# Attention and channel mix in one kernel: the token mixtures as a four-chunk difference, scalings by mu spread over three engines, and a four-chunk addition

## The chip, the core and the metric

The kernel runs on one core of a Trainium2 chip. Its engines are TensorE (PE, with its weight loads shown as PEld), VectorE (DVE), ScalarE (ACT), GpSimd (POOL) and SyncE (SP), which here only issues DMAs. The metric is the device time of one execution in microseconds (us), as the median of several runs. One further execution was recorded by the profiler; every row of a profile below is from such an execution, and its times count from the first instruction.

## What is computed

First a windowed attention over 4 batches, 8 heads, 768 positions and heads of 64 (each query sees the 128 latest keys and the first 4), then a channel mix on the attention's output x, which has 512 channels:

```python
x_prev = np.concatenate([np.zeros((B, 1, D)), x[:, :-1, :]], axis=1)
xk = mu_k * x + (1.0 - mu_k) * x_prev
xr = mu_r * x + (1.0 - mu_r) * x_prev
k = np.maximum(xk @ w_k, 0.0)          # 512 -> 1024
v = k * k @ w_v                        # 1024 -> 512
r = 1.0 / (1.0 + np.exp(-(xr @ w_r)))  # 512 -> 512
return r * v
```

The change concerns xk and xr, the two mixtures. Both equal `x_prev + mu * (x - x_prev)`, so one difference serves both.

## The kernel before

The work is cut into 12 units u of 256 positions, three to a batch. A unit goes through four stages.

- `prepare(u)` casts q, k and v from float32 to bf16 (`kb`, `qb`, `vb`, lines 645 to 652 and 711) and transposes q and k, on TensorE for the earlier units with an evacuation from PSUM (lines 678 to 697), and by DMA for the later ones.
- `attend(u)` works on four pairs of heads. For each pair TensorE computes scores (L786), ScalarE the exponential `e` (L858), VectorE multiplies `e` by the 0/1 mask (L872), TensorE forms values and the row sums (L891), and VectorE divides (reciprocal L905, product `x` L908). The first four keys have small matmuls of their own (L755, L829, L844).
- `mix(u)` transposes x so that channels lie on partitions (four chunks of 128 channels): TensorE L932, copy to `xt` L941. It then builds the mixtures in two halves of two chunks. For each half VectorE computes `td`, the difference of `xt` and `xt` shifted by one position, on two chunks at once (L959, 128x512), and then, for each chunk and for each of xk and xr, one fused `scalar_tensor_tensor`: td times mu, where mu is one float32 scalar per partition, plus the shifted `xt` (L970, 128x256).
- `ffn(u)` runs the three products: keys (L1022, four chunks of xk summed into PSUM), relu on ScalarE or VectorE (L1032, L1036) and its square (L1044), the gate from xr (L1053) with a tanh (L1059), and the value product (L1071; the very last tile in pieces, L992), whose result VectorE multiplies by the gate (L1080) for the store. `ffn(u - 1)` is written after `mix(u)`.

All operations are entered into a `Plan` with a cost and due rank, and are numbered as they are entered. `ORDER` holds for each engine the numbers in the order in which that engine executes them, written out in full. `CHOICE` says for operations that more than one engine could do (casts, copies out of PSUM, relu, the shape of the sink matmuls) which one does it; an operation that is not in the table runs on its default engine. `schedule()` walks through the five orders with the costs, lags and DMA rates written in the code, only to fix the order of emission, the buffer of each tile, and where TensorE gets filler matmuls on a tile of zeros (L1095, L1098) while it waits during the first 22 us. Each engine executes its own list in order, so an instruction that waits holds up everything behind it on that engine. Loads, DMA transposes and stores are issued in the order of the SP list; the float32 weights come by five loads of 1024 KB (two for w_k, one for w_r, two for w_v) and each is cast to bf16 in parts (L606, L610, L612).

Tiles come from pools of a fixed number of buffers: three of `td` (two chunks each), four of `xk`, three of `xr`, four PSUM banks for everything but the scores.

Of the kernel before, what the change touches and what calls it, by code (L numbers as in the profile page):

```python
# [18 lines left out]
    79: "ACT", 80: "POOL", 81: "POOL", 83: "POOL", 84: "ACT", 86: "ACT", 88: "ACT",  # L19
    89: "POOL", 91: "DVE", 95: "POOL", 97: "DVE", 101: "DVE", 134: "POOL", 137:  # L20
    "POOL", 140: "ACT", 141: "DVE", 143: "DVE", 159: "PE/full", 171: "PE/tiles", 182:
    "POOL", 185: "POOL", 191: "POOL", 193: "DVE", 194: "ACT", 220: "DVE", 241:
    "PE/tiles", 253: "PE/full", 264: "DVE", 270: "POOL", 276: "DVE", 289: "DVE", 297:
    "DVE", 351: "POOL", 353: "DVE", 354: "POOL", 356: "DVE", 387: "DVE", 404:
    "PE/full", 416: "PE/tiles", 427: "POOL", 429: "POOL", 432: "POOL", 434: "POOL",
    440: "DVE", 484: "PE/tiles", 496: "PE/tiles", 509: "POOL", 586: "POOL", 591:
    "POOL", 643: "PE/tiles", 655: "PE/full", 668: "POOL", 672: "POOL", 721:
    "PE/tiles", 733: "PE/tiles", 746: "POOL", 752: "ACT", 753: "ACT", 823: "POOL",
    825: "POOL", 827: "POOL", 830: "DVE", 832: "DVE", 876: "PE/tiles", 888: "PE/full",
    899: "POOL", 903: "POOL", 908: "ACT", 952: "PE/tiles", 964: "PE/full", 983: "DVE",  # L30
    1019: "DVE", 1023: "DVE", 1031: "DVE",
# [7 lines left out]
BIAS = ()  # L39

# [19 lines left out]
SWITCH = 100.0  # L60
# [30 lines left out]
    ),  # L91
    "DVE": (
# [25 lines left out]
    ),  # L118
    "ACT": (
# [32 lines left out]
class Plan:  # L152

    SEM = 60.0
# [170 lines left out]
def kernel(  # L332
# [61 lines left out]
    def dve(n, rate=1.04):  # L394
        return 64.0 + rate * n
# [759 lines left out]
```

## Time and profile before

| | us |
|---|---|
| median of 3 runs | 170.01 (169.42 to 171.2) |
| span of the profiled execution, first to last instruction | 167.0 |
| TensorE busy | 155.6 |
| VectorE busy | 151.0 |
| ScalarE busy | 119.1 |
| GpSimd busy | 41.0 |
| the 96 fused mixture instructions, L970, busy | 45.8 |
| the 24 differences, L959, busy | 10.5 |

The profiled execution has no separate time of its own on record, only its span; the median of the runs lies 3.0 us above that span, which is what lies around the instructions. TensorE's granted clock was 1.000.

How to read it: "busy" is the time in which at least one instruction of an engine is under way. Matmuls and VectorE instructions overlap their successors at the ends, so the duration of one instruction is longer than its share of the engine. The share is the step, the difference between the starts of two neighbours in the timeline when the second one did not wait.

### The profile page before, as it was taken

Reading aid. Unit: us, or ns where it says so; the run is one execution under the profiler, and the core shown is the slowest. Engines: PE = TensorE matmul, PEld = TensorE weight load, DVE = VectorE, ACT = ScalarE, POOL = GpSimd, SP = SyncE. Lnnn points to the kernel's source line nnn. Section 1 sums busy time; section 2 is a strip of 40 time slices with the busy share of each in tenths; the row PEclk is TensorE's granted clock in tenths of the full one; section 3 lists DMA queues with packets and bytes.
Section 4 is the critical chain, followed back from the end, with each engine's and each line's share of the span. In section 5 each row is a group of like instructions: output and inputs, shape, how many; then the busy total and the mean of one; then the engine's idle time right before and its main releaser. Section 6 shows DMA issues by size and latency. Waiting matters only on the chain.

```text
span 167.0 us, 4752 instructions
## 1 busy us (share of the span) xinstructions
PE 155.6 (93%) x1865; PEld 103.7 (62%) x1884; DVE 151.0 (90%) x382; ACT 119.1 (71%) x193; POOL 41.0 (25%) x72
## 2 busy tenths in 40 slices
PE   7687998999999999999989999999999999999991
PEld 2456676755667686667566686575765774678441
DVE  6189999999999999999999999999999999895941
ACT  4497988898898987987779898878597492125020
POOL 5664223200555351621820030250030000000000
PEclk9999999999999999999999999999999999999999
DMA  4999999999999989999968969996998251311033
GB/s 142 237 338 384 294 253 327 390 388 274 223 299 206 226 221 257 173 236 194 220 161 185 228 160 170 194 206 150 233 217 153 82 140 42 126 66 63 0 138 113
DMA packets 72277, 33.85 MB, mean 203 GB/s; under 512 B 61624, under 2 KB 63936, under 8 KB 72256
## 3 DMA queue, kind: packets, MB, share of 16 engines
q1 hardware_dynamic: 72240, 33.56, 84.9%
q8 instruction: 14, 0.23, 0.6%
q14 instruction: 7, 0.06, 0.2%
q10 hardware_dynamic: 16, 0.00, 0.0%
HBM read 24.12 MB, written 6.29 MB: 182 GB/s over the span
## 4 chain that ended last, share of the span: by engine, by line
DVE 45%; PE 43%; issue 5%; DMA 3%; SPq 1%; ACT 1%; DVEq 0%; ACTq 0%
PE bank L1071 14%; PE bank L1022 12%; DVE e L872 10%; PE bank L1053 7%; DVE xr L970 6%; DVE xk L970 5%; DVE x L908 5%; DVE kk L1044 4%; PE bank L891 3%; DMA vs<-in_v_dram 3%; DVE ob L1080 3%; DVE td L959 3%; PE sc L786 2%; DVE rec L905 2%; PE bank L932 1%
## 5 line engine op out<-in xcount | busy, mean ns | idle before, releaser
L1022 PE MATMUL bank<-xk,wk_sb 128*128 128x256 bf16 x384 | 51.4, 273 | 1.1 <-DVE x L908 0.5
L858 ACT ACTIVATE e<-sc 128x1024 bf16<-128x1024 f32 (+1 forms) x48 | 44.7, 963 | 5.1 <-PE sc L786 5.0
L1071 PE MATMUL bank<-wv_h,kk 128*128 128x512 bf16 x175 | 44.3, 379 | 0.4
L1022 PEld LDWEIGHTS <-wk_sb 128*128 128x128 bf16 x384 | 35.4, 98 | 10.1 <-issue 1.2
L1032 ACT ACTIVATE rl<-bank 128x512 bf16<-128x512 f32 x42 | 24.9, 607 | 15.9 <-PE bank L1022 14.0
L872 DVE TENSOR_TENSOR e<-e,mask 128x1024 bf16<-128x1024 bf16 (+1 forms) x48 | 32.5, 691 | 0.1
L1071 PEld LDWEIGHTS <-kk 128*128 128x128 bf16 x184 | 17.0, 98 | 15.4 <-DVE kk L1044 0.2
L1053 PE MATMUL bank<-wr_sb,xr 128*128 128x512 bf16 x86 | 23.8, 380 | 0.7 <-DVE x L908 0.2
L970 DVE SCALAR_TENSOR_TENSOR xr<-td,mu_all,xt 128x256 bf16<-128x256 bf16 x48 | 23.4, 502 | 0.0
L970 DVE SCALAR_TENSOR_TENSOR xk<-td,mu_all,xt 128x256 bf16<-128x256 bf16 x48 | 22.4, 496 | 0.1
L1059 ACT ACTIVATE th<-bank 128x512 f32<-128x512 f32 x24 | 14.4, 607 | 9.7 <-PE bank L1053 9.6
L908 DVE TENSOR_TENSOR x<-bank,rec 128x256 bf16<-128x256 f32 x48 | 19.5, 418 | 0.7
L1044 DVE TENSOR_TENSOR kk<-rl 128x512 bf16<-128x512 bf16 x48 | 19.7, 427 | 0.3 <-ACT rl L1032 0.2
L891 PE MATMUL bank<-vb,e 128*128 128x65 bf16 x352 | 16.8, 194 | 1.7 <-DVE e L872 1.4
L891 PEld LDWEIGHTS <-e 128*128 128x128 bf16 x352 | 14.2, 97 | 5.5 <-DVE e L872 2.8
L1080 DVE SCALAR_TENSOR_TENSOR ob<-th,bank 128x512 f32<-128x512 f32 x23 | 15.7, 681 | 2.1 <-ACT th L1059 1.3
L711 POOL CAST vb<-vs 128x512 bf16<-128x512 f32 x15 | 12.7, 854 | 15.4 <-DMA vs<-in_v_dram 15.3
L1053 PEld LDWEIGHTS <-xr 128*128 128x128 bf16 x96 | 8.8, 97 | 8.2 <-issue 0.4
L941 ACT COPY xt<-bank 128x512 bf16<-128x512 bf16 x17 | 10.0, 588 | 4.4 <-PE bank L932 4.4
L786 PE MATMUL sc<-qt,kt 64*64 64x128 bf16 (+4 forms) x496 | 12.8, 226 | 0.2
L786 PEld LDWEIGHTS <-kt 64*64 64x64 bf16 (+1 forms) x496 | 9.2, 106 | 4.0 <-issue 2.1
L649 POOL CAST qb<-qs 128x512 bf16<-128x512 f32 x5 | 3.7, 755 | 28.1 <-PE bank L1022 13.0
(83 smaller groups left out, 166.0 us busy)
## 6 DMA issues: line engine op xcount, KB each, us to landing
vs<-in_v_dram SPq DMA_DIRECT2D x24, 256.0 KB, 5.2
out_dram<-ob SPq DMA_DIRECT2D x23, 256.0 KB, 2.7
ks<-in_k_dram SPq DMA_DIRECT2D x16, 256.0 KB, 5.4
qs<-in_q_dram SPq DMA_DIRECT2D x7, 512.0 KB, 6.0
qs<-in_q_dram SPq DMA_DIRECT2D x10, 256.0 KB, 4.7
ks<-in_k_dram SPq DMA_DIRECT2D x4, 512.0 KB, 8.6
w<-in_moe_w_k_dram SPq DMA_DIRECT2D x2, 1024.0 KB, 10.4
w<-in_moe_w_v_dram SPq DMA_DIRECT2D x2, 1024.0 KB
```

What stands on the lines that cost most here:

```text
L786: nc.tensor.matmul(out=sc[keys, a, o0 + f0 - q0:o0 + f1 - q0], lhsT=lhs[rows, keys], rhs=qs[rows, f0:f1], start=u not in BIAS, stop=True, ...
L858: nc.scalar.activation(out=buf[ek][:, :, lo:], in_=buf[sck][:, :, lo:], func=AF.Exp, scale=scale)
L872: nc.vector.tensor_tensor(out=at, in0=at, in1=m, op=ALU.mult)
L891: nc.tensor.matmul(out=o[:, g, a, :], lhsT=e[:, a, e0:e0 + 128], rhs=rhs, start=(T == 0 and i == 0), stop=(i == len(blocks) - 1), skip_gro ...
L908: P.op("DVE", dve(256), lambda ok=ok, rk=rk, c=c: nc.vector.tensor_tensor(out=buf["x", u][:, :, 128 * c:128 * c + 128].rearrange("p g (a d ...
L970: nc.vector.scalar_tensor_tensor(out=buf[key][:, c, :], in0=buf[tk][:, i, :], scalar=mu[w][:, c:c + 1], in1=xt[:, c, t0 - 1:t0 + 255], op0 ...
L1022: nc.tensor.matmul(out=ps[:, i, :], lhsT=wk_sb[:, c, 128 * f:128 * f + 128], rhs=xk[:, c, :], start=(c == 0), stop=(c == NC - 1), skip_gro ...
L1032: nc.scalar.activation(out=buf[rk], in_=buf[psk].rearrange("p (i t) -> p i t", i=2), func=AF.Relu)
L1044: P.op("DVE", dve(512, 0.52), lambda f2=f2, rk=rk: nc.vector.tensor_tensor(out=buf["kk", u][:, 2 * f2:2 * f2 + 2, :], in0=buf[rk], in1=buf ...
L1053: nc.tensor.matmul(out=buf[psk], lhsT=buf["xr", u][:, c, 128 * g:128 * g + 128], rhs=wr_sb[:, c, :], start=(c == 0), stop=(c == NC - 1))
L1071: nc.tensor.matmul(out=buf[psk], rhs=wv_h[:, f, :], lhsT=buf["kk", u][:, f, 128 * g:128 * g + 128], start=(f == 0), stop=(f == NF - 1))
L1080: P.op("DVE", dve(512), lambda psk=psk, tk=tk, bk=bk: nc.vector.scalar_tensor_tensor(out=buf[bk], in0=buf[tk], scalar=1.0, in1=buf[psk], o ...
```

## The change

1. **The mixtures.** In units 1 to 10 (`WIDE`) the difference is one instruction on four chunks (128x1024) in place of two on two chunks. The fused instruction is gone in all units. In its place each chunk of xk and xr is scaled by its mu alone (128x256, bf16 in and out): eight scalings a unit, each on VectorE, ScalarE or GpSimd as `CHOICE` says. An addition on VectorE then adds the shifted `xt` in place, on four chunks at once (128x1024), one for xk and one for xr. Units 0 and 11 keep their halves: two differences, eight scalings and four additions on two chunks (128x512).
2. **The buffers.** `td` has two buffers of four chunks in place of three of two.
3. **The tables.** `CHOICE` and all five orders are replaced. Counted over the tables, VectorE has 39 of the 96 scalings, ScalarE 24 and GpSimd 33. Of the operations that were there before, VectorE takes on 5 more copies of `xt`, 3 more casts of `vb`, 4 of `kb`, 5 of `qb`, 2 more evacuations of `qt`, 2 more relus, and has one weight cast fewer; ScalarE gives away the 5 copies of `xt`, 2 evacuations of `qt`, 2 relus and 8 casts of `kb` and `qb`, and keeps as many weight and `vb` casts as before; GpSimd has 3 fewer casts of `vb`, 1 fewer of `kb` and `qb` together, and 1 more weight cast. TensorE's operations are the same, in a new order; 3 pairs of sink matmuls go from whole rows to tiles of 64. SP has the same 115 operations in a new order.
4. **The planner's constants.** Costs, lags and the price of a wait in `schedule()` are new. They change no instruction by themselves.

Switches that are off (`FUSED`, `FP`) bring nothing into the program. The core of the diff:

```diff
-    pool("td", 3, [128, 2, 256], BF16)
+    pool("td", 2, [128, NC, 256], BF16)
...
-            P.op("DVE", dve(512, 0.5), lambda cs=cs, tk=tk: nc.vector.tensor_tensor(
-                out=buf[tk], in0=xt[:, cs, t0:t0 + 256],
-                in1=xt[:, cs, t0 - 1:t0 + 255], op=ALU.subtract), r, port=True,
-                take=[("td", tk)], reads=made + prev, writes=[tk])
+            if u in WIDE and half == 0:
+                continue
+            n = NC if wide else 2
+            c0 = 0 if wide else 2 * half
...
+            last = xt[:, c0:c0 + n, t0 - 1:t0 + 255]
+            P.op("DVE", dve(256 * n, 0.52), lambda tk=tk, c0=c0, n=n, last=last:
+                 nc.vector.tensor_tensor(
+                     out=buf[tk][:, 0:n, :], in0=xt[:, c0:c0 + n, t0:t0 + 256], in1=last,
+                     op=ALU.subtract), r, port=True,
+                 take=[("td", tk)], reads=made + prev, writes=[tk])
             for w, name in enumerate(("xk", "xr")):
...
-                        nc.vector.scalar_tensor_tensor(
+                    def scaled(by, w=w, i=i, c=c, tk=tk, key=key):
+                        if by == "ACT":
+                            return lambda: nc.scalar.activation(
+                                out=buf[key][:, c, :], in_=buf[tk][:, i, :], func=AF.Copy,
+                                scale=mu[w][:, c:c + 1])
+                        engine = nc.vector if by == "DVE" else nc.gpsimd
+                        return lambda: engine.tensor_scalar(
                             out=buf[key][:, c, :], in0=buf[tk][:, i, :],
-                            scalar=mu[w][:, c:c + 1],
-                            in1=xt[:, c, t0 - 1:t0 + 255], op0=ALU.mult,
-                            op1=ALU.add)
+                            scalar1=mu[w][:, c:c + 1], scalar2=None, op0=ALU.mult)
...
+                P.op("DVE", dve(256 * n, 0.52), lambda key=key, c0=c0, n=n, last=last:
+                     nc.vector.tensor_tensor(
+                         out=buf[key][:, c0:c0 + n, :], in0=buf[key][:, c0:c0 + n, :], in1=last,
+                         op=ALU.add), r + 4 * w, port=True, hold=[key],
+                     reads=[key + ("y", c0 + i) for i in range(n)] + made + prev,
+                     writes=[key + (c0 + i,) for i in range(n)])
```

The start of the SP order, with what the numbers stand for (q, k and v of a unit are 512 KB each, some in two issues; `wk0` and `wk1` are the two halves of w_k, 1024 KB each):

```
before: q0 k0 q0 k0 v0 v0 k1 q1 q2 wk0 wk1 v1 v1 k2 v2 wr v2 wv0 k3 wv1 q3 q4 ...
after:  q0 k0 q1 k0 q0 k1 v0 v0 q2 k2 v1 q3 v1 k3 wk0 wk1 v2 v2 wr wv0 q4 wv1 ...
```

More of the change, by code (lines that the diff above doesn't have):

```diff
@@ L18 @@
 CHOICE = {
[L19 to L30, printed above, removed]
@@ new lines @@
+    269: "POOL", 272: "DVE", 277: "DVE", 278: "POOL", 281: "DVE", 282: "ACT", 287:
+    "DVE", 289: "DVE", 292: "POOL", 293: "POOL", 294: "POOL", 297: "POOL", 298:
+    "ACT", 299: "POOL", 351: "POOL", 354: "DVE", 360: "POOL", 364: "ACT", 366:
+    "DVE", 370: "POOL", 371: "POOL", 372: "POOL", 375: "ACT", 377: "POOL", 378:
+    "POOL", 386: "DVE", 411: "PE/full", 434: "POOL", 436: "POOL", 439: "POOL", 447:
+    "DVE", 451: "POOL", 452: "POOL", 456: "ACT", 457: "ACT", 458: "ACT", 467: "DVE",
+    515: "POOL", 520: "POOL", 522: "POOL", 526: "ACT", 531: "DVE", 533: "DVE", 538:
@@ L32 @@
+    "PE/full", 978: "PE/full", 993: "POOL", 995: "POOL", 996: "POOL", 999: "DVE",
+    1002: "POOL", 1004: "POOL", 1005: "POOL", 1013: "DVE", 1017: "DVE", 1021: "DVE",
+    1037: "DVE",
 }
@@ L39 @@
 BIAS = ()
+WIDE = range(1, 11)
+FUSED = ()
+FP = ()
 LOW = -30000.0
@@ L152 @@
 class Plan:
-    SEM = 60.0
+    SEM = 40.0
+    LAG = {"PE": 163.0, "DVE": 83.0, "ACT": 114.0, "POOL": 60.0, "SP": 90.0}
     def __init__(self):
@@ L313, in schedule @@
                 if whole:
[L314 to L315 removed]
+                    at[j] = max(at[j], clock["PE"] if ops[j]["engine"] == o["engine"] == "PE"
+                                else end + self.SEM)
                 else:
@@ L654, in cast @@
                     in_=buf[raw][:, hs, :, :])
-            P.op("ACT", act(512), cast(nc.scalar.copy), rank + half,
-                 alts={"ACT": (act(512), cast(nc.scalar.copy), False),
-                       "DVE": (dve(512, 0.52), cast(nc.vector.tensor_copy), True),
-                       "POOL": (650.0, cast(nc.gpsimd.tensor_copy), True)},
-                 take=[] if half else [(name + "b", rk)],
-                 hold=[raw] + ([rk] if half else []),
-                 reads=[(name, u, half), "table"],
-                 writes=[rk + (half,)])
+            whole = (name, u) in FP
+            if not whole:
+                P.op("ACT", 515.0, cast(nc.scalar.copy), rank + half,
+                     alts={"ACT": (515.0, cast(nc.scalar.copy), False),
+                           "DVE": (341.0, cast(nc.vector.tensor_copy), True),
+                           "POOL": (600.0, cast(nc.gpsimd.tensor_copy), True)},
+                     take=[] if half else [(name + "b", rk)],
+                     hold=[raw] + ([rk] if half else []),
+                     reads=[(name, u, half), "table"],
+                     writes=[rk + (half,)])
             if by_dma(name, u):
@@ L672, in prepare, with transpose32 @@
                 continue
+            def transpose32(half=half, psk=psk, raw=raw):
+                ps = buf[psk].rearrange("p (j t) -> p j t", j=4)
+                for j in range(4):
+                    nc.tensor.transpose(out=ps[:, j, :], identity=ident32,
+                                        in_=octets(buf[raw])[:, :, 4 * half + j, :])
             def transpose(half=half, psk=psk, rk=rk, name=name):
@@ L685, in transpose, with evacuate @@
                         in_=buf[rk][:, j % 2, 2 * c:2 * c + 2, :].rearrange("p a d -> p (a d)"))
-            P.op("PE", 225.0, transpose, rank + half, lag=PE_LAG, take=[("bank", psk)],
-                 reads=["ident", rk + (half,)], writes=[psk], hold=[rk])
-            def evacuate(copy, half=half, psk=psk, key=key, name=name):
+            if whole:
+                P.op("PE", 1000.0, transpose32, rank + half, take=[("bank", psk)], mode=4,
+                     reads=["ident", (name, u, 0), (name, u, 1)], writes=[psk], hold=[raw])
+            else:
+                P.op("PE", 225.0, transpose, rank + half, take=[("bank", psk)],
+                     reads=["ident", rk + (half,)], writes=[psk], hold=[rk])
+            def evacuate(copy, half=half, psk=psk, key=key, name=name, whole=whole):
                 if octet(name, u):
@@ new lines, in mix @@
+            wide = u in WIDE
+            n = NC if wide else 2
+            c0 = 0 if wide else 2 * half
+            tk = ("td", u, half)
+            hs = range(2) if wide else (half,)
+            made = [("xt", b % 2, T, i, g) for i in hs for g in range(2)]
+            prev = [("xt", b % 2, T - 1, i, 1) for i in hs] if T else ["edges"]
+            last = xt[:, c0:c0 + n, t0 - 1:t0 + 255]
[4 more added lines that the diff above has]
+                 take=[("td", tk)], reads=made + prev, writes=[tk])
```

115 lines of the change are left out of this document (73 added, 42 removed), and 144 rows, old and new, of the table ORDER.

## The prediction

> **What bounds the kernel now.** I read the chain of waits first, for which engine sets the end, then the chain in order of time, for where that changes.
>
> ```profile
> DVE 45%; PE 43%; issue 5%; DMA 3%; SPq 1%; ACT 1%; DVEq 0%; ACTq 0%
> ```
>
> ```profile
> 92.28 0.61 DVE ob L1080
> 92.93 0.60 PE bank L1022 x4
> ...
> 162.54 0.66 PE bank L992 x4
> ```
>
> VectorE and TensorE share the chain, but in time: up to about 92 us it runs almost wholly over VectorE, after it almost wholly over TensorE, to 163.2 us. So time taken off VectorE is worth something in the first part only. The table of busy time by stage comes next; its columns are length, then PE, PEld, DVE, ACT, POOL, the clock, the DMA share and GB/s.
>
> ```profile
> 10.00:20.00 10.00, 8.51 (x130) 5.77 (x127) 9.51 (x24) 8.81 (x14) 4.01 (x8) 1.00 1.08 366
> 20.00:40.00 20.00, 18.89 (x236) 13.12 (x235) 19.91 (x49) 18.07 (x30) 3.44 (x4) 1.00 1.03 333
> ...
> sum 167.00, PE 155.61 PEld 103.75 DVE 151.00 ACT 119.12 POOL 40.98; mean PE 14.15 PEld 9.43 DVE 13.73 ACT 10.83 POOL 3.73
> ```
>
> VectorE is busy 19.91 of 20 us, but TensorE 18.89 too. How much room TensorE has left is the main question, and busy time does not answer it, since matmuls overlap. I take steps (start to start) from its timeline and counts from the groups:
>
> ```profile
> 19.89 1.91 PE L1022 MATMUL bank<-xk,wk_sb 128*128 128x256 bf16 x16
> ```
>
> ```profile
> 101.95 1.89 PE L1071 MATMUL bank<-wv_h,kk 128*128 128x512 bf16 x8
> 103.67 0.60 PE L1022 MATMUL bank<-xk,wk_sb 128*128 128x256 bf16 x4
> 104.11 1.03 PE L1053 MATMUL bank<-wr_sb,xr 128*128 128x512 bf16 x4
> 104.97 0.39 PE L932 MATMUL bank<-ident,x 128*128 128x128 bf16 x4
> 105.20 1.03 PE L1053 MATMUL bank<-wr_sb,xr 128*128 128x512 bf16 x4
> ...
> 119.25 0.53 PE L786 MATMUL sc<-qt,kt 64*64 64x192 bf16 x24
> 119.71 0.36 PE L891 MATMUL bank<-vb,e 128*128 128x65 bf16 x6
> 119.91 1.03 PE L1071 MATMUL bank<-wv_h,kk 128*128 128x512 bf16 x3
> ```
>
> ```profile
> L1022 PE MATMUL bank<-xk,wk_sb 128*128 128x256 bf16 x384 | 51.4, 273 | 1.1 <-DVE x L908 0.5 <-DVE wk_sb L612 0.2 <-ACT xt L941 0.2
> L1071 PE MATMUL bank<-wv_h,kk 128*128 128x512 bf16 x175 | 44.3, 379 | 0.4
> L1053 PE MATMUL bank<-wr_sb,xr 128*128 128x512 bf16 x86 | 23.8, 380 | 0.7 <-DVE x L908 0.2
> L891 PE MATMUL bank<-vb,e 128*128 128x65 bf16 x352 | 16.8, 194 | 1.7 <-DVE e L872 1.4 <-ACT th L1059 0.2
> L786 PE MATMUL sc<-qt,kt 64*64 64x128 bf16 (+4 forms) x496 | 12.8, 226 | 0.2
> ```
>
> Keys step 0.44/4 = 0.11 us, so 384 take 42.2. Products step 1.72/8 and gates 0.86/4 = 0.215; the code issues 184 and 96 of them (some records are missing above), 60.2 us. Transposes step 0.23/4 = 0.058; 26 operations of `prepare` and 22 of `mix`, four each, make 11.0. Scores step 0.46/24 = 0.019, 9.5 us; values 0.20/6 = 0.033, 11.7 us. The last tile and the sinks I put at 7. Together about 142 us of real work in a span of 167: 25 us are lost. By the orders, what precedes the first keys at 19.89 us is 48 transposes (2.8), the scores of two units (1.8), 24 value matmuls (0.8) and a few sinks (0.4), some 5.8 us; the rest of TensorE's time there is waiting and filler on the tile of zeros, so 14.1 us go there. From 163.2 us to the end it is 3.8. So only 25 - 14.1 - 3.8, about 7 us, lies in gaps between 20 and 163 us. **That is all that a faster VectorE can win**, apart from the head.
>
> **The change, part by part.** VectorE's steps:
>
> ```profile
> 28.48 1.26 DVE L970 SCALAR_TENSOR_TENSOR xr<-td,mu_all,xt 128x256 bf16<-128x256 bf16 x1
> ...
> 101.58 0.42 DVE L959 TENSOR_TENSOR td<-xt 128x512 bf16<-128x512 bf16 x1
> 101.91 0.48 DVE L970 SCALAR_TENSOR_TENSOR xr<-td,mu_all,xt 128x256 bf16<-128x256 bf16 x1
> ...
> 104.83 0.68 DVE L872 TENSOR_TENSOR e<-e,mask 128x1024 bf16<-128x1024 bf16 x1
> 105.43 0.47 DVE L970 SCALAR_TENSOR_TENSOR xk<-td,mu_all,xt 128x256 bf16<-128x256 bf16 x1
> 105.83 0.47 DVE L970 SCALAR_TENSOR_TENSOR xr<-td,mu_all,xt 128x256 bf16<-128x256 bf16 x1
> ```
>
> *Removed:* 96 fused instructions at a step of 0.40 (105.43 to 105.83) are 38.0 us, 24 differences at 0.33 (101.58 to 101.91) 7.9: 45.9 us.
>
> *Added, wide:* 10 differences and 20 additions of 1024 columns, two bf16 inputs in SBUF like `e`, whose step is 0.60: 18.0. Four differences and eight additions of 512 at 0.33: 4.0.
>
> *Added, scalings on VectorE:* no row shows one. 39 instructions of 256 columns cannot cost more than the 0.33 of a difference twice as wide, nor less than a quarter of it, 0.08 (half the columns, one tensor read in place of two). I take 0.20, nearer to the row: 7.8 us (3.1 to 12.9). [...]
>
> *Sum of the mixtures on VectorE:* 45.9 - 29.8 = 16.1 us less. *Moved to VectorE:* 17 casts and copies of 512 columns at 0.33 (as the difference, equally wide) 5.6, four evacuations and relus from PSUM 2.4 (an estimate: 0.60, as `e`, which is twice as wide but lies in SBUF), one weight cast of 1024 columns fewer at 0.60: 7.4 us more.
>
> *GpSimd* gets 33 scalings and loses three casts. Its timeline shows what that costs the others:
>
> ```profile
> 17.10 1.20 POOL L612 CAST wk_sb<-w 128x1024 bf16<-128x1024 f32 x1 [1.24 <-DMA w<-in_moe_w_k_dram]
> ...
> 28.38 1.09 POOL L612 CAST wr_sb<-w 128x1024 bf16<-128x1024 f32 x1 [2.87 <-DMA w<-in_moe_w_r_dram]
> ...
> 42.38 0.61 POOL L645 CAST qb<-qs 128x512 bf16<-128x512 f32 x1
> ...
> 59.74 2.41 POOL L711 CAST vb<-vs 128x512 bf16<-128x512 f32 x1 [3.94 <-DMA vs<-in_v_dram]
> ```
>
> A cast of 512 columns takes 0.61 alone and 2.41 at 59.74; the fused instruction at 28.48, which runs into the weight cast of 28.38, takes 1.26 in place of 0.47. Each blocks the other. A scaling of half the width holds GpSimd about 0.3 to 0.6 us; if each costs VectorE from 0 to its whole 0.6, 33 of them cost 0 to 20 us. I take 0.1 each, 3.3 us, since most of the 0.61 casts pass beside neighbours of normal length, as this one at 28.48 does not. **Net on VectorE: 16.1 - 7.4 - 3.3, about 5 us less** (bounds: 13 less to 16 more).
>
> *ScalarE* gets 24 scalings. The nearest row is the exponential of the sinks, also 256 columns:
>
> ```profile
> L762 ACT ACTIVATE es<-bank 128x256 bf16<-128x256 f32 x8 | 3.2, 396 | 0.6 <-PE bank L755 0.6
> ```
>
> At 0.40 that is 9.6 us; it gives away 17 operations of 512 columns, which cannot be cheaper than that one each, 6.8 us or more. Net 0 to 3 us on 119 of 167: hidden behind the idle third of ScalarE in the late stages.
>
> *The head.* In the new SP order v1, k2, q3 and k3, 2 MB, are issued ahead of w_k. At the 366 GB/s of 10 to 20 us that is 5.5 us, so the weights that the cast at 17.10 waited for land near 22.6 and the first keys move from 19.9 to about 25. In exchange the transposes of unit 3, the first scores of unit 2 and the values of unit 1 stand ahead of the keys: 76 transposes 4.4, scores 2.7, values 1.9, sinks 0.6, together 9.6 us by 25 us. Before, 5.8 us and then 5 us of nearly full work stood there: 10 to 11. So the head costs about 1 us (bounds -2 to +3), and two units then lie ready at once.
>
> *Waits and buffers.* Two `td` buffers hold two units; a unit's `td` is free after its last xr scaling, so a difference two units later can wait for that, about 24 us later in time: nothing. *Tail:* value products of units 8, 9 and 10 stand between and behind the last keys, as cover for the last mixture; I take 0.
>
> *Sum.* 5 us off VectorE spread over 20 to 163 us; half of that time (72 of 143 us) VectorE sets the pace, 2.5 us; the other half gives nothing. The new orders must also spend the 1 us of the head; I let the gaps of the second part (3 us of the 7) pay that, since the extra cover by attention work is there. Span 167.0 - 2.5 = 164.5; with the 3.0 us around the span, by which the median stands above this profile, **167.5 us**.
>
> **The rivals.**
>
> *A, additions wait for GpSimd (slower).* 21 of the 28 additions have at least one scaling on GpSimd before them, and VectorE is in order: if that scaling is late, all masks and divisions behind the addition wait. Between a difference and its xk addition the new VectorE list has as little as five to seven instructions (units 1, 8, 10, 11), 1.5 to 2.4 us by the steps above. For it: GpSimd's scalings stand in one queue with casts that wait for DMAs (3.94 us at 59.74), and one stretched cast is 1.8 us late. Against: most additions have 4 to 10 us of other work ahead. If a third of the 21 wait 1.2 us, 8 us come back on VectorE, 3 more than were saved; with the 1 us of the head, and again half of it on the path, 170.0 + 4/2 = 172.0 us. It decides from 5/21 = 0.25 us per addition. [...]
>
> *B, TensorE alone is the bound (no change).* The 7 us of gaps come from switching, records and semaphores, and VectorE's relief changes none. Then 170.0, less at most 1: 169.3. For it: 18.89 of 20 us busy even while VectorE leads the chain.
>
> [...]
>
> **How the numbers follow.** A measurement of this kernel can tell about 1% from no change, so faster means below 168.3 and slower above 171.7. Forecast 0.38 (its own range 166 to 168.9, nearly all of it faster), C 0.14, B 0.23, A 0.25. Faster 0.50, same 0.25, slower 0.25. The range goes from C to A: 164.0 to 172.5.
>
> **What would show it.** Right: VectorE busy near 146 us, no row of an addition waiting over 1 us for POOL, first L1022 near 25 us and TensorE's keys, products and gates without gaps after 30 us. Wrong: additions at the head of the waits; GpSimd scalings of over 1 us; a first key matmul after 27 us; VectorE still near 150; or filler and idle time of TensorE past 30 us.

## The result, and the profile after

The changed kernel takes 172.67 us (median of 20 executions, 170.89 to 175.63), the kernel before 170.02 beside it (20 executions, 168.91 to 172.38): a ratio of 1.0146 (95% interval 1.0115 to 1.0177), so slower by 1.5%. The ratios here and below leave out executions of more than 1.5% above the fastest of their own series, the medians leave out none. The forecast was 167.5 with a range of 164.0 to 172.5; the time lies 0.2 us past its upper end. The first profile of the changed kernel was taken while TensorE's granted clock was lowered (0.97 in the mean, 0.50 from 24 to 32 us), so the lines below are from another execution of the same kernel (span 170.9 us, clock 1.000); the kernel before had a span of 167.0.

The two traces are not equally typical. In 99 further executions of the kernel before the median span is 168.5, and in 38 of the changed kernel 170.7, so the usual growth is about 2.2 us and not the 3.9 between these two. Time and span of one execution lie 1.7 to 2.9 us apart; the 3.0 us that were put down to what lies around the instructions come in part from a quick execution in the profile before. The sum, which starts from the median, does not suffer from it.

The chain of waits, shares of the span by engine:

```profile
PE 42%; DVE 28%; issue 12%; DMA 6%; POOL 4%; ACT 3%; SPq 2%; DVEq 0%; POOLq 0%; ACTq 0%
```

VectorE's part fell from 45 to 28%, and "issue", DMA and POOL took most of what it left. The next lines are the busy times in two stages, 20 to 40 us and 40 to 160 us (columns as before: length, PE, PEld, DVE, ACT, POOL, clock, DMA share, GB/s), first the kernel before, then the changed one:

```profile
20.00:40.00 20.00, 18.89 (x236) 13.12 (x235) 19.91 (x49) 18.07 (x30) 3.44 (x4) 1.00 1.03 333
40.00:160.00 120.00, 117.44 (x1443) 78.99 (x1459) 115.52 (x288) 85.83 (x142) 26.84 (x37) 1.00 0.84 172
```

```profile
20.00:40.00 20.00, 15.10 (x260) 11.96 (x261) 19.76 (x46) 17.61 (x30) 11.44 (x13) 1.00 1.03 334
40.00:160.00 120.00, 117.36 (x1416) 77.72 (x1415) 107.96 (x269) 88.75 (x151) 49.20 (x56) 1.00 0.82 171
```

These four lines hold most of the answer. From 40 to 160 us VectorE works 7.6 us less, as the change meant it to, and TensorE is exactly as busy as before, 117.4 of 120. From 20 to 40 us VectorE is as full as ever, GpSimd works 8 us more, and TensorE loses 18.89 - 15.10 = 3.8 us. The span grew by 3.9 between these traces.

TensorE's timeline shows where most of it goes (start, length, work, and in brackets the idle time before it with what ended it):

```profile
21.25 0.40 PE L710 MATMUL bank<-ident,qb 128*128 128x128 bf16 x4 [1.43 <-DVE qb L669]
...
27.69 0.29 PE L791 MATMUL bank<-qt,ksink 128*32 128x256 bf16 x4 [1.62 <-DVE x L944]
27.92 0.40 PE L710 MATMUL bank<-ident,kb 128*128 128x128 bf16 x4
28.15 1.04 PE L1096 MATMUL bank<-xk,wk_sb 128*128 128x256 bf16 x8
```

The first keys come at 28.15 us (19.89 before, about 25 forecast), and both waits are for VectorE. GpSimd's and then VectorE's timeline at that place say what VectorE was doing:

```profile
19.09 0.93 POOL L1035 TENSOR_SCALAR xk<-td,mu_all 128x256 bf16<-128x256 bf16 x1 [1.44 <-DVE td L1004]
20.00 0.92 POOL L1035 TENSOR_SCALAR xr<-td,mu_all 128x256 bf16<-128x256 bf16 x1
...
22.89 1.07 POOL L669 CAST qb<-qs 128x512 bf16<-128x512 f32 x1
24.66 2.03 POOL L636 CAST wk_sb<-w 128x1024 bf16<-128x1024 f32 x2 [0.71 <-DMA w<-in_moe_w_k_dram]
27.74 1.04 POOL L636 CAST wk_sb<-w 128x1024 bf16<-128x1024 f32 x1 [1.05 <-DMA w<-in_moe_w_k_dram]
```

```profile
23.61 0.42 DVE L944 TENSOR_TENSOR x<-bank,rec 128x256 bf16<-128x256 f32 x1
...
24.50 0.28 DVE L1035 TENSOR_SCALAR xk<-td,mu_all 128x256 bf16<-128x256 bf16 x1
24.69 0.24 DVE L941 RECIPROCAL rec<-bank 128x4 f32<-128x4 f32 x2
24.85 0.93 DVE L1035 TENSOR_SCALAR xk<-td,mu_all 128x256 bf16<-128x256 bf16 x1
25.70 1.60 DVE L1049 TENSOR_TENSOR xk<-xk,xt 128x512 bf16<-128x512 bf16 x2
27.22 0.75 DVE L944 TENSOR_TENSOR x<-bank,rec 128x256 bf16<-128x256 f32 x2
27.89 1.43 DVE L908 TENSOR_TENSOR e<-e,mask 128x1024 bf16<-128x1024 bf16 x1
```

While GpSimd casts w_k (24.66 to 26.69, and from 27.74) VectorE's scaling takes 0.93 in place of 0.28, the two additions 1.60 (0.75 in e12 below, where no cast stands beside them), and the mask 1.43 in place of 0.68; the product `x` at 23.61, which reads a PSUM bank, takes its usual 0.42 beside the cast of 22.89. With those casts on ScalarE, in e10 below, the same scaling takes 0.26, the two additions 0.76 and the mask 0.68. So it is GpSimd's casts that stretch these instructions; by what mechanism, no run shows.

The GpSimd scalings themselves, as groups (busy, then mean ns of one), and two neighbours of which the second did not wait:

```profile
L1035 POOL TENSOR_SCALAR xr<-td,mu_all 128x256 bf16<-128x256 bf16 x19 | 20.9, 1103 | 25.5 <-DVE td L1004 12.1 <-DVE rec L941 7.9 <-PE bank L1096 3.9
L1035 POOL TENSOR_SCALAR xk<-td,mu_all 128x256 bf16<-128x256 bf16 x14 | 14.8, 1058 | 7.3 <-DVE td L1004 7.3
```

```profile
115.63 0.92 POOL L1035 TENSOR_SCALAR xr<-td,mu_all 128x256 bf16<-128x256 bf16 x1 [3.88 <-PE bank L1096]
116.53 0.92 POOL L1035 TENSOR_SCALAR xk<-td,mu_all 128x256 bf16<-128x256 bf16 x1
```

A scaling on GpSimd steps by 0.90 us, not 0.3 to 0.6. VectorE's, at 94.26 and 94.45, step by 0.19, as taken:

```profile
94.26 0.28 DVE L1035 TENSOR_SCALAR xr<-td,mu_all 128x256 bf16<-128x256 bf16 x1
94.45 0.28 DVE L1035 TENSOR_SCALAR xk<-td,mu_all 128x256 bf16<-128x256 bf16 x1
94.65 0.69 DVE L1049 TENSOR_TENSOR xr<-xr,xt 128x1024 bf16<-128x1024 bf16 x1
```

### The profile page after: what moved, and what is told of

Read it like the earlier page. It is cut to its first block, busy times and chain, and to the rows that moved or that the text cites. A ratio compares the mean times of both kernels' runs of the same rounds, so it can differ in the third digit from the quotient of the medians.

```text
span 172.3 us, 4799 instructions
## 1 busy us (share of the span) xinstructions
PE 158.1 (92%) x1868; PEld 105.2 (61%) x1887; DVE 146.3 (85%) x363; ACT 119.8 (69%) x200; POOL 74.1 (43%) x102
## 4 chain that ended last, share of the span: by engine, by line
PE 42%; DVE 29%; issue 12%; DMA 6%; POOL 4%; ACT 2%; SPq 2%; DVEq 0%; POOLq 0%; ACTq 0%
PE bank L1096 15%; PE bank L1145 11%; DVE e L908 8%; PE bank L1127 6%; DMA qs<-in_q_dram 6%; DVE x L944 4%; DVE kk L1118 3%; PE bank L927 3%; DVE ob L1154 3%; PE sc L822 2%; DVE td L1004 2%; POOL xr L1035 2%; DVE xk L1035 2%; PE bank L968 1%; DVE xk L1049 1%
## 5 line engine op out<-in xcount | busy, mean ns | idle before, releaser
L1145 PE MATMUL bank<-wv_h,kk 128*128 128x512 bf16 x171 | 43.1, 379 | 0.6
L1096 PEld LDWEIGHTS <-wk_sb 128*128 128x128 bf16 x384 | 37.3, 101 | 10.3 <-issue 2.7
L908 DVE TENSOR_TENSOR e<-e,mask 128x1024 bf16<-128x1024 bf16 (+1 forms) x48 | 33.8, 717 | 0.2 <-ACT e L894 0.2
L1106 ACT ACTIVATE rl<-bank 128x512 bf16<-128x512 f32 x40 | 23.3, 604 | 14.4 <-PE bank L1096 13.5
L1035 POOL TENSOR_SCALAR xr<-td,mu_all 128x256 bf16<-128x256 bf16 x19 | 20.3, 1073 | 26.3 <-DVE td L1004 12.8
L1035 POOL TENSOR_SCALAR xk<-td,mu_all 128x256 bf16<-128x256 bf16 x14 | 15.1, 1085 | 8.6 <-DVE td L1004 8.6
L747 POOL CAST vb<-vs 128x512 bf16<-128x512 f32 x12 | 10.2, 856 | 13.3 <-DMA vs<-in_v_dram 7.9
L822 PE MATMUL sc<-qt,kt 64*64 64x128 bf16 (+3 forms) x496 | 13.2, 232 | 1.0 <-ACT kt L728 1.0
L977 ACT COPY xt<-bank 128x512 bf16<-128x512 bf16 x12 | 6.9, 586 | 6.1 <-PE bank L968 6.0
L673 POOL CAST kb<-ks 128x512 bf16<-128x512 f32 x9 | 6.7, 744 | 10.1 <-DMA ks<-in_k_dram 10.0
```

Source lines behind the costliest of these rows:

```text
L822: nc.tensor.matmul(out=sc[keys, a, o0 + f0 - q0:o0 + f1 - q0], lhsT=lhs[rows, keys], rhs=qs[rows, f0:f1], start=u not in BIAS, stop=True, ...
L908: nc.vector.tensor_tensor(out=at, in0=at, in1=m, op=ALU.mult)
L1035: return lambda: engine.tensor_scalar(out=buf[key][:, c, :], in0=buf[tk][:, i, :], scalar1=mu[w][:, c:c + 1], scalar2=None, op0=ALU.mult)
L1096: nc.tensor.matmul(out=ps[:, i, :], lhsT=wk_sb[:, c, 128 * f:128 * f + 128], rhs=xk[:, c, :], start=(c == 0), stop=(c == NC - 1), skip_gro ...
L1106: nc.scalar.activation(out=buf[rk], in_=buf[psk].rearrange("p (i t) -> p i t", i=2), func=AF.Relu)
L1145: nc.tensor.matmul(out=buf[psk], rhs=wv_h[:, f, :], lhsT=buf["kk", u][:, f, 128 * g:128 * g + 128], start=(f == 0), stop=(f == NF - 1))
```

## The experiments

Theories after the result. T1: the slow GpSimd scalings cost it, through VectorE and late additions (rival A). T2: VectorE's relief is worth nothing, since TensorE sets the pace (rival B), and the later first keys are a pure loss. T3: the longer way to a mixture (difference, scaling, addition) comes too late for the early units. Each ratio is against the kernel before on the same chip in the same session, with its 95% interval.

### GpSimd's share

**e1: the changed kernel again**

> The changed kernel unchanged, for a second profile beside the same day's runs of the kernel before. In the first profile the first keys came at 28.6 us (19.9 before), at a granted clock of 0.74 between 20 and 40 us, and TensorE's gaps after the first keys added up to about 7 us as before. Theory H (the head): without that dip the keys start 5 us or more later than before, with only about 4 us more work done ahead of them, so the head alone costs 2 to 4 us and the gaps after it are as before. Theory G (GpSimd): the gaps after the first keys are 2 us or more larger than before. Both expect about 172.3 in time.

172.48 us, ratio 1.0189 (1.0131 to 1.0247). The second profile above is this one's.

**e2 and e15: the 33 scalings of GpSimd on VectorE**, at their places by planned time.

```diff
-    145: "POOL", 148: "POOL", 158: "POOL", 211: "POOL", 292: "POOL", ...
+    (these 33 scalings stay on their default, VectorE; ORDER follows)
```

> The changed kernel with the 33 scalings of GpSimd moved to VectorE, each at the place in VectorE's list that corresponds to its planned start; nothing else moved. VectorE gets 33 x 0.20 = 6.6 us of work, and loses the waits behind GpSimd's scalings, which took 0.9 us each in the trace in place of the 0.3 to 0.6 that I had priced. Theory G: the blocking and the late additions cost more than the 6.6 us: 170 to 171, clearly below the changed kernel. Theory H: the loss sits ahead of the first keys and GpSimd's scalings are covered: 172 to 174, the same as the changed kernel or slower.

> The changed kernel with its 33 GpSimd scalings on VectorE, once more, as the partner of the filled version on the same chip. Both theories: ratio 1.010 to 1.016, mean clock below 0.995 in more than half of the executions.

1.0134 (1.0080 to 1.0188) in the first session, 1.0035 (0.9988 to 1.0083) in another. The two intervals hardly overlap, though the medians of all executions stand closer, 1.011 and 1.009 times those of before; so this alone does not say how much is GpSimd's. It does say that without any GpSimd scaling the kernel is not faster than before.

**e5: plain copies on GpSimd in place of its scalings**

```diff
+                        if by == "POOL":
+                            return lambda: nc.gpsimd.tensor_copy(
+                                out=buf[key][:, c, :], in_=buf[tk][:, i, :])
```

> The changed kernel with GpSimd's 33 scalings replaced by plain copies of the same 128x256 bf16 (these chunks of xk and xr are left unscaled, so the output is another one). A GpSimd cast of twice the width took 0.61 us alone, so a copy should take 0.3 to 0.4 in place of the 0.9 of a scaling by a per-partition mu. Theory G (the price of GpSimd's scalings is what makes the change slow): 169.5 to 170.5, 2 us or more below the changed kernel. Theory H (the head): at most 0.7 below it, 171.5 to 172.5; the one pair of these scalings ahead of the first keys is all that helps the head.

1.0035 (0.9991 to 1.0079); first keys at 25.55 us; span 167.8. A copy of the same 128x256 steps by 0.34 us (78.98 to 79.32):

```profile
78.98 0.40 POOL L1035 COPY xr<-td 128x256 bf16<-128x256 bf16 x1 [6.81 <-DVE td L1004]
79.32 0.40 POOL L1035 COPY xk<-td 128x256 bf16<-128x256 bf16 x1
```

and the stages are

```profile
20.00:40.00 20.00, 17.25 (x275) 12.95 (x276) 19.50 (x49) 18.30 (x33) 9.30 (x11) 1.00 1.00 330
40.00:160.00 120.00, 118.06 (x1414) 78.12 (x1413) 107.82 (x270) 86.90 (x148) 29.78 (x56) 1.00 0.87 173
```

With GpSimd at the price that the prediction had taken for it, VectorE's relief is the same, the head still loses 18.89 - 17.25 = 1.6 us, and 40 to 160 us gives back 0.6. So the forecast fails even with GpSimd as cheap as assumed, and that is T2. How much T1 adds, these traces do not say: e12 below, where 29 of the 33 are still multiplications, has 17.41 and 117.80 in TensorE's column, nearly the same as e5.

**e9: GpSimd multiplies by a constant**

```diff
+                        if by == "POOL":
+                            return lambda: nc.gpsimd.tensor_scalar(
+                                out=buf[key][:, c, :], in0=buf[tk][:, i, :], scalar1=0.5,
+                                scalar2=None, op0=ALU.mult)
```

> The changed kernel, but GpSimd's 33 scalings multiply by the constant 0.5 instead of the column of mu (so those chunks are mixed with another weight; everything else is as before). Theory 'it is the scalar read from SBUF for each partition that makes the GpSimd scaling slow': with a constant the step falls from 0.90 us to near the plain copy's 0.34, GpSimd's busy time from 74 to about 52 to 56 us, and the ratio to the kernel before from 1.019 to about 1.004. Rival 'tensor_scalar itself is slow on GpSimd, whatever its scalar': step near 0.9 us, ratio 1.015 to 1.02.

1.0256 (1.0153 to 1.0359, from four executions); the step is 0.81 (84.91 to 85.72), nearer to 0.90 than to the copy's 0.34:

```profile
84.91 0.85 POOL L1035 TENSOR_SCALAR xr<-td 128x256 bf16<-128x256 bf16 x1 [8.69 <-DVE td L1004]
85.72 0.85 POOL L1035 TENSOR_SCALAR xk<-td 128x256 bf16<-128x256 bf16 x1
```

It is the `tensor_scalar` on GpSimd, here a multiplication, that is slow; reading mu for each partition adds only about 0.1.

**e12, e13, and again e16 to e18: head or all along?** Copies in the four GpSimd scalings of units 0 and 1, or in the other 29.

```diff
+                        if by == "POOL" and u < 2:     # e12, e17;  u >= 2 in e13, e18
+                            return lambda: nc.gpsimd.tensor_copy(
+                                out=buf[key][:, c, :], in_=buf[tk][:, i, :])
```

> The changed kernel, but the four GpSimd scalings of the first two units are plain copies (those chunks stay unscaled); the other 29 are as they are. Theory 'the slow GpSimd scalings cost in the head': the first keys come at 25.5 instead of 28.15 us, as when all 33 were copies, and the ratio falls from about 1.017 to 1.005. Rival 'they cost all along, by holding VectorE and by late additions': keys earlier, but the ratio stays above 1.012.

> The opposite: the 29 GpSimd scalings of the other units are plain copies (those chunks stay unscaled), the four of the first two units are as they are. Theory 'in the head': first keys at 28 us, ratio 1.012 to 1.018. Rival 'all along': ratio about 1.005 to 1.008 in spite of keys at 28 us.

> The changed kernel itself, as the partner of the two halves on the same chip. Both theories: ratio 1.012 to 1.020, first keys at 28 us or later.

> Copies in place of the four GpSimd scalings of the first two units. Theory 'in the head': ratio 0.010 or more below the changed kernel's beside it, keys at 25.5 us. Theory 'all along': less than 0.005 below it, whenever the keys come.

> Copies in place of the 29 GpSimd scalings of the other units. Theory 'in the head': less than 0.005 below the changed kernel's ratio. Theory 'all along': 0.010 or more below it, with the first keys still at 28 us or later.

| | first session | second session |
|---|---|---|
| changed kernel | | e16 1.0102 (1.0065 to 1.0139) |
| copies in the first two units | e12 1.0081 (1.0027 to 1.0135) | e17 1.0133 (1.0075 to 1.0191) |
| copies in the others | e13 0.9996 (0.9955 to 1.0038) | e18 1.0023 (0.9976 to 1.0071) |

I had looked for the cause in the four early scalings and was wrong: they cannot be told from nothing (e17 lies above e16). With copies in the 29 others the ratio is about 0.8% lower (e16 less e18; e12, with these 29 slow, lies as far above e13), or 0.6% by the medians of all executions. That lies between what the two theories had for e18 (under 0.5%, 1.0% or more), and its keys were to stay at 28 us but came at 25.99. So T1 "all along" is likely, not shown: e12 and e18, both with early keys, have spans of 168.7 and 168.6, so part of the 0.8% can be the head's (next section). The trace of e1 shows one place at which a late scaling costs time: at 107.41 an addition waits 1.44 us for GpSimd, whose scaling stands behind a cast that waited for a load, and then TensorE waits 1.62 us for VectorE's output rows.

```profile
108.85 0.70 DVE L1049 TENSOR_TENSOR xr<-xr,xt 128x1024 bf16<-128x1024 bf16 x1 [1.44 <-POOL xr L1035]
```

```profile
112.35 0.92 PE L1096 MATMUL bank<-xk,wk_sb 128*128 128x256 bf16 x7 [1.62 <-DVE ob L1154]
```

With copies (e5) the same waits are 1.1 and 1.2 us, so the load behind which GpSimd stands makes most of them. Where the rest of the 0.8% goes is open.

### The head

The profiles of e12 and e17 are of one and the same kernel, and their first keys lie 2.7 us apart. In e12, TensorE's timeline and then VectorE's at the addition of the first xk:

```profile
25.54 1.05 PE L1099 MATMUL bank<-xk,wk_sb 128*128 128x256 bf16 x8 [0.18 <-POOL wk_sb L636]
```

```profile
23.33 0.75 DVE L1052 TENSOR_TENSOR xk<-xk,xt 128x512 bf16<-128x512 bf16 x2
```

In e17, the same two views:

```profile
28.20 1.04 PE L1099 MATMUL bank<-xk,wk_sb 128*128 128x256 bf16 x8
```

```profile
25.22 1.13 DVE L1038 TENSOR_SCALAR xk<-td,mu_all 128x256 bf16<-128x256 bf16 x1
...
26.59 0.75 DVE L1052 TENSOR_TENSOR xk<-xk,xt 128x512 bf16<-128x512 bf16 x2
```

The same kernel gave early and late keys twice more: e15 and e2 at 26.38 and 28.03 us, e18 and e13 at 25.99 and 30.25.

In both e12 and e17, GpSimd starts on w_k at 24.2 to 24.4 us. In e12 the first mixtures are done by 24.1, ahead of it; in e17, whose first scores came 0.67 us later (8.46 for 7.79), they run into it. The spans are 168.7 and 170.9. So the new order of the head stands on an edge: a half-microsecond at the start becomes two at the end of the head. Of the kernels with this head, the profiles with keys at 25.5 to 26.4 us (e5, e12, e15, e18) have spans of 167.8 to 168.7, those with keys at 28.0 to 28.4 (e1, e2, e16, e17) of 169.5 to 170.9, and those with keys at 28.6 to 30.3 (the first profile, e9, e13), all at a mean clock of 0.97, of 172.3 to 173.5.

The half-microsecond comes from TensorE. Filler and first scores in e12, then in e17:

```profile
7.47 0.38 PE L1172 MATMUL bank<-warm 128*128 128x512 bf16 x1
7.79 0.50 PE L822 MATMUL sc<-qt,kt 64*128 64x256 bf16 x8
```

```profile
7.89 0.63 PE L1172 MATMUL bank<-warm 128*128 128x512 bf16 x1
8.46 0.82 PE L822 MATMUL sc<-qt,kt 64*128 64x256 bf16 x8
```

In e12 the filler of this shape takes 0.63 us at 5.96 and 0.38 at 7.47; in e17 it still takes 0.63 at 7.89, and the first four transposes at 0.39 in place of 0.63 come at 10.29. So TensorE comes to its shorter times later in e17, although the clock column reads 1.00 for its first 20 us. In the 14 profiles in the changed orders the two always go together: first scores of 0.50 us with keys at 25.5 to 26.4 (the four named), first scores of 0.60 to 0.82 with keys at 27.7 or later (the other ten, among them all three profiles of the changed kernel itself). No run here sets that moment on its own, so it is not shown that it decides the head.

**e10: w_k's three GpSimd casts on ScalarE; e11: q and k of the fourth unit after w_k**

```diff
-    79: "POOL", 80: "POOL", 82: "POOL",
+    79: "ACT", 80: "ACT", 82: "ACT",
```

```diff
-after:  ... v0 v0 q2 k2 v1 q3 v1 k3 wk0 wk1 ...
+e11:    ... v0 v0 q2 k2 v1 v1 wk0 wk1 q3 k3 ...
```

> The changed kernel, but the three w_k casts that GpSimd does between 24.6 and 28.8 us are done by ScalarE at the same place of the work. Theory 'in the head VectorE is held by GpSimd': VectorE's scaling of 0.93, additions of 0.8 each and mask of 1.43 us in that stretch fall back to 0.28, 0.42 and 0.68, the first keys come at 26.5 to 27 instead of 28.15, and the ratio falls by about 0.006 to 0.010, to 1.009 to 1.013. Rival 'the keys come late because w_k lands late and ScalarE is busy with the exponentials': keys stay within 0.5 us of 28.15, ratio stays at 1.015 to 1.022.

> The changed kernel, but q and k of the fourth unit are requested after w_k instead of ahead of it, as in the kernel before, with that unit's preparation put some 3 us later on the other engines. Theory 'the arrival of w_k sets the first keys': w_k lands 2 to 3 us earlier, the first keys come at about 25.5 to 26, and the ratio falls to about 1.005. Rival 'the chain difference, scaling, addition and what GpSimd does beside it sets them': w_k lands earlier, the keys stay within 1 us of 28.15, and the ratio stays at 1.015 or rises, since the fourth unit comes later as well.

1.0313 (1.0221 to 1.0404) and 1.0368 (1.0305 to 1.0430). In e10 the additions are done at 25.89 in place of 27.30 and the mask takes 0.68 us, as expected, but the keys come at 27.67 and the time rises: TensorE's clock was 0.50 from 24 to 28 us, and ScalarE had the casts on top of its exponentials. In e11 GpSimd starts on w_k at 21.87, but the keys stay at 28.25, since TensorE waits 1.1 us for a cast of q that waited for its load. Both mend one wait and bring another; the w_k load alone does not set the first keys.

**e14: idle matmuls in TensorE's gaps of the head** (in the version of e2)

```diff
+            for wide in {273: (4, 1), 171: (2,), 279: (1,), 243: (4, 2)}.get(i, ()):
+                b = min(free["bank"])
...
+                order.append(("fill", self.pools["bank"][b[1]], wide))
```

> The changed kernel with its 33 GpSimd scalings on VectorE, and 14 units of idle matmuls on zeros put into TensorE's gaps between 19.7 and 28 us. Theory 'the gap in the head costs TensorE its clock': the granted clock stays at 1.00 in the slices from 20 to 30 us, the mean clock is 1.00 in nearly all executions, and the median falls by 0.7 to 1.5 us against the same version unfilled. Rival 'the dip is not from the gap': slices of 0.5 to 0.8 remain in half of the executions, median within 0.5 us or later by the matmuls that come in the way.

1.0309 (1.0271 to 1.0348). A miss by its own making: the filler took the PSUM bank that was planned to be free and had to wait for it, so it came after the gap and not in it:

```profile
23.25 1.65 PE L1167 MATMUL bank<-warm 128*128 128x512 f32 x2 [1.59 <-ACT xt L972]
```

It tells nothing about the clock.

### The mixtures in the old orders

Here the orders are those of the kernel before, so w_k comes early and the keys lead.

**e6: a control.** The program of before with the changed planner constants and `td` buffers of four chunks.

```diff
-    pool("td", 3, [128, 2, 256], BF16)
+    pool("td", 3, [128, NC, 256], BF16)
```

> Control: the kernel before (its orders, its choices, its fused mixtures) written with the changed kernel's planner constants and three td buffers of four chunks, which alter only the order of emission, buffer numbers and filler matmuls. Both theories: the same as the kernel before, 169.3 to 170.5. If it is slower, part of what the run of the mixtures in the old orders (177.7) lost is due to this and not to the mixtures.

0.9961 (0.9927 to 0.9995), keys at 19.65: the constants and three buffers of that width cost nothing.

**e4, e8, e7: the new mixtures in these orders, every scaling on VectorE:** wide in units 1 to 10 (e4), halves everywhere (e8), wide in units 4 to 10 and fused elsewhere (e7). `td` has two buffers of four chunks in e4, three in e7 and e8.

```diff
-WIDE = ()
-FUSED = (0, 1, 2, 3, 4, 5, 6, 7, 8, 9, 10, 11)
+WIDE = (4, 5, 6, 7, 8, 9, 10)      # e4: range(1, 11)   e8: ()
+FUSED = (0, 1, 2, 3, 11)           # e4: ()             e8: ()
```

> The mixtures alone: all orders and choices of the kernel before, with the wide differences and additions, and all 96 scalings on VectorE at the places of the fused instructions. By the measured steps VectorE does 45.9 - 18.0 - 4.0 - 96 x 0.20 = 4.7 us less work. If VectorE's relief is worth half of itself, as the prediction put it: 167.5 to 168.5. If TensorE alone sets the pace (rival B): 169.5 to 170.5. If the longer way from difference to addition makes the keys late: above 171.

> The kernel before with difference, scaling and addition in halves of two chunks in every unit, all on VectorE, all orders and choices of before. VectorE: 24 x 0.33 + 96 x 0.20 + 48 x 0.33 = 43.0 us in place of 45.9. If the width of four chunks (the difference has to wait for all four pairs of heads) is what made the run of the mixtures in the old orders slow: 169.5 to 171. If it is the addition that stands at the end of the chain of scalings: 174 or more.

> The kernel before with the new mixtures in units 4 to 10 only (wide, all scalings on VectorE), fused ones in units 0 to 3 and 11, all orders and choices of before. VectorE saves 7/12 of 4.7 us plus what the halves would have cost, about 3 us, after 50 us into the span. If VectorE's relief is worth half of itself: 168 to 169. If TensorE sets the pace: 169.5 to 170.5. If the loss of 8 us with all units wide came from the first units alone (nothing of this kernel is ahead of the keys yet, so a later xk delays them at once): no loss here; if the longer way from difference to addition costs in every unit: 172 or more.

e4 1.0487 (1.0432 to 1.0542), e8 1.0335 (1.0264 to 1.0405), e7 1.0026 (0.9992 to 1.0060). No GpSimd scaling is in any of them. In e4 the first keys come at 19.41 as before, and then TensorE waits for VectorE (its waits up to 60 us):

```profile
PE bank L1083 <- DVE xk L1036: 2.1, 1, 2.1
PE bank L914 <- DVE x L931: 1.5, 1, 1.5
PE bank L955 <- DVE x L931: 0.8, 1, 0.8
```

The way to a mixture is longer, and the wide one starts only when all four chunks are transposed. In the early units TensorE has nothing else to do, so it shows; that is T3. From unit 4 on it is hidden (e7). That e7 brings no gain either does not test T2: its profile, from one of the longer executions (span 170.8), shows VectorE busy 153.5 us, against 151.0 before and 153.0 in e6, so the relief of about 3 us that was expected is not there.

**e3: the other half of the trade.** The kernel before with the first 22 loads in the order of after, all else as it was.

```diff
-q0 k0 q0 k0 v0 v0 k1 q1 q2 wk0 wk1 v1 v1 k2 ...
+q0 k0 q1 k0 q0 k1 v0 v0 q2 k2 v1 q3 v1 k3 wk0 wk1 ...
```

> The kernel before with one thing changed: the first 22 entries of the SP order are those of the changed kernel (the same 22 loads; v1, k2, q3 and k3 ahead of w_k). TensorE's order stays, so its keys stand where they stood and simply wait for the weights. Theory H: the keys start 5 us later and nothing fills the time: 173 to 175.6. If loads in the head are not what TensorE waits for: 170 to 171.

1.0522 (1.0477 to 1.0566); keys at 25.55, span 176.5. In the old orders the new start of the loads costs 8.3 us (178.17 for 169.84). Not all of it is w_k: the second q comes later as well (its cast starts at 9.22 us, 6.82 before), and TensorE stands still for it from 5.95 to 9.89 us, with a clock of 0.50 from 10 to 15 us.

```profile
9.89 0.61 PE L681 MATMUL bank<-ident,qb 128*128 128x128 bf16 x4 [3.94 <-ACT qb L650]
```

The new orders, which suit these loads and put attention of the next units ahead of the keys, win most of that back; they do not make it a gain.

## Why the prediction was wrong, point by point

- **The mixtures on VectorE: right.** Scalings at 0.19 (0.20 taken). VectorE's busy time is 146.0, forecast 146.
- **"A scaling of half the width holds GpSimd about 0.3 to 0.6 us": failed.** 0.90. It was sized from a cast's 0.61 per 512 columns, that is by columns, and a copy of the kind does follow that (0.34); the multiplication does not (e5, e9). It is worth at most about 0.8% of the time (e16 against e18), of which the head's two kinds of execution may be a part.
- **"If each costs VectorE 0.1": about right in sum.** VectorE is 146.0 us busy with scalings on GpSimd and 143.3 with copies, 2.7 us more for the 33 multiplications than for copies. With none on GpSimd (e2) it is 149.2; less 33 scalings of 0.19 that makes 142.9, so an estimated 3.1 us in all, forecast 3.3. So the busy sum was right although the length was wrong; what it missed are the waits behind a late scaling.
- **"Half of that time VectorE sets the pace, 2.5 us": failed, and with it the whole gain.** The relief is there, 7.6 us from 40 to 160 us, but TensorE was busy 117.4 of 120 us before it and 117.4 after. In the chain of before VectorE led to 92 us; that share said which engine ended last, not how much TensorE would win if it did not. My own count of TensorE's work had left 7 us of gaps, and I gave VectorE a third of them. The view that bears on this I had not read: TensorE's waits in the kernel before, cut to 30 to 164 us, are five, 1.7 us in all (columns: who waited for whom, us in total, times, longest):

```profile
PE bank L844 <- DVE ob L1080: 0.6, 1, 0.6
PE bank L1022 <- DVE x L908: 0.5, 1, 0.5
PE bank L844 <- DVE rl L1036: 0.2, 1, 0.2
PE bank L1053 <- DVE x L908: 0.2, 1, 0.2
PE bank L891 <- ACT th L1059: 0.2, 1, 0.2
```

  All of TensorE's idle time in that stretch is 134 - 130.78 = 3.2 us; the rest of the 7 us lies inside its busy time, where the profile shows no wait for VectorE. So 2.5 us were hardly there to win, and e5, with the same relief, won 0.6 from 40 to 160 us. From 20 to 40 us, where VectorE was really the pace, it is as full as before (19.76 of 20), since casts were moved onto it and GpSimd's weight casts stand beside it.
- **"So the head costs about 1 us", paid from later gaps: mis-sized, and this is the larger term.** The stage from 20 to 40 us loses 3.8 us in e1, with keys at 28.15 where about 25 was forecast, and still 1.6 in e5, with keys at 25.55; and no gap after 40 us paid for it. The load came later than the 22.6 us of the sum: GpSimd's first w_k cast starts at 24.66 in e1, at once after its wait for the load. What was also missed is that the first mixtures and the w_k casts on GpSimd now fall on the same two microseconds.
- **ScalarE hidden, buffers and tail nothing: right as far as seen.** ScalarE is 119.7 busy (119.1 before). After 160 us TensorE is idle for 3.4 us in both traces. No run tests two buffers alone (e6 has three); in e1 one difference waits 0.4 us for a GpSimd scaling.
- **The rivals.** A gave 172.0, and 172.67 was measured; that it is so near is luck. Additions wait for GpSimd three times, 2.1 us in all of e1, not seven times 1.2. Of the signs of being wrong, GpSimd scalings over 1 us (1.06 and 1.10 in the mean) and a first key after 27 us came true. B's mechanism, no gain from VectorE's relief, is the one the traces bear out; with copies for the slow scalings the time is that of before (e5 170.71 for 170.47, e18 170.76 for 170.25), a little above B's 169.3. Slow scalings and a bound by TensorE do not exclude each other, and I had put A and B side by side as if they did. No run shows the relief behind the lower end of the range, 164.0 (C): VectorE's scalings step by 0.19, they lengthen beside a cast on GpSimd (0.93 for 0.28 in e1), and e5 won 0.6 us from 40 to 160 us.
- **Open:** how much of the 0.8% of e16 against e18 is the 29 later scalings' own and where they lose it outside the one place shown; what sets the moment at which TensorE's filler goes from 0.63 to 0.38 us, and with it, perhaps, the first keys. No version tried beats the kernel before by more than the measurement can tell; e6, its control, is at 0.9961.

## What to carry to other kernels

Before giving work to a freer engine, look for a row of that very operation on that engine: a copy's price is no price for a multiplication there (0.34 against 0.81 and 0.90 us on GpSimd here). And before counting a relief as gain, sum what the other engine waits for in that stage: 1.7 us of waits in 3.2 us of idle time leave hardly room for 2.5, whatever share the relieved engine has in the chain. A new order that gets ahead of a load's casts by half a microsecond can miss that in part of the executions (e12 and e17, keys at 25.54 and 28.20); look at two profiles of one kernel before explaining a head by its code.

## What the runs showed of the hardware

- GpSimd, 128x256 bf16 to bf16: copy 0.34 us a step, `tensor_scalar` with a constant 0.81, with a scalar per partition 0.90. VectorE 0.19, ScalarE 0.51 long.
- TensorE's granted clock fell to 0.50 for some microseconds after a thin stretch of work in some executions, as in the first profile of the changed kernel:

```profile
20.00:22.00 2.00, 0.67 (x28) 0.57 (x28) 2.00 (x5) 1.89 (x4) 1.00 (x2) 1.00 1.05 388
22.00:24.00 2.00, 1.03 (x40) 0.74 (x28) 2.00 (x4) 2.00 (x4) 1.36 (x2) 0.77 1.05 385
24.00:26.00 2.00, 1.96 (x28) 1.77 (x32) 1.93 (x8) 1.11 (x3) 1.33 (x2) 0.50 1.14 337
26.00:28.00 2.00, 1.45 (x32) 1.10 (x32) 2.00 (x5) 1.75 (x4) 0.98 (x2) 0.50 1.00 171
```

  TensorE is busy 0.67 and 1.03 of 2 us, then the clock (the third column from the end) is 0.50. So it was in e10, with 0.63 and 1.44 busy and then 0.50 from 24 to 28 us, and in e3, where 3.9 us without a matmul were followed by 0.50 from 10 to 15 us. In e1 the same stretch (0.75 and 1.41 busy) passed at 1.00, and so did 26 to 28 us with 0.38. So a thin stretch was not always followed by 0.50; what decides it, no run here shows. Executions with a mean clock of 0.99 or less: 22 of 38 of the changed kernel, 1 of 99 of the kernel before, whose thinnest four microseconds from 10 to 28 us (11 to 15) hold 2.6 us of TensorE's work. The five executions of the changed kernel at 1.00 in the first comparison have a median of 171.40, still 1.4 us above before, so the slowing does not rest on the clock.
